# Windowed attention and a two-layer MLP on one core: the first two batches in thirds of 192 tokens, the first chunk up-projected in two column halves, the last 64 tokens loaded ahead of w_in

## The chip, the cores and the metric

The kernel runs on one core of one Trainium2 chip. The metric is the device time of one execution in microseconds (us). TensorE is called PE here, VectorE DVE, ScalarE ACT, GpSimd POOL, and SyncE, whose queue issues nearly all DMAs, SP. PE has two rows in the profile: PE for matmuls and PEld for loads of weights.

## What is computed

Attention over 8 batches, 8 heads, 576 tokens and 64 elements per head, in float32 inputs and outputs. Heads 0 to 3 see a plain window of the last 32 tokens; heads 4 to 7 see a dilated one, every fourth of the last 128. The rows of all heads of a token, side by side (512 wide), then pass an up-projection, a leaky ReLU and a down-projection.

```python
    mask_plain = (rel >= 0) & (rel < window)                                   # window = 32
    mask_dil = (rel >= 0) & (rel < window * dilation) & (rel % dilation == 0)  # dilation = 4
    masks = np.stack([mask_plain if h < H // 2 else mask_dil for h in range(H)], axis=0)
    scores = np.where(masks[None, :, :, :], scale * np.matmul(q, k.transpose(0, 1, 3, 2)), -1e9)
    attn = softmax(scores)
    x = np.matmul(attn, v).transpose(0, 2, 1, 3).reshape(B * S, H * D)         # 4608 x 512
    h = x @ w_in                                                              # 512 x 2048
    return np.maximum(0.01 * h, h) @ w_out                                     # 2048 x 512
```

## The kernel before

**Who sets the order.** No engine's order is written by hand. Every piece of work is a task with an engine (or a choice of engines), a cost, a latency, what it depends on, and a due time or rank (`add`, `dma`, lines 68 to 78). `_Plan.run` (line 85) plays the tasks through a small model and emits each engine's instructions in the order that comes out; for loads the model has a transfer rate by packet size (`took`, 252) and extra lateness (`LATE`). At run time each engine takes its instructions strictly in that order and waits on semaphores, so a task that is not ready holds up all that is behind it. Where the model leaves PE without work early on, filler matmuls on zeros are put in (line 1595; eight more stand at the very start, 1489).

**Loads.** `FIRST` (line 21) ranks the early loads. `b` and `v` are q with k, and v, of one half of the heads of batch 0 (dilated heads first), `i` one of eight blocks of w_in (128 rows by 1024 columns, 512 KB), `o` one of eight blocks of w_out, `0` the last 64 tokens of batch 0, `c`, `y` and `1` the same three things for batch 1. The loads of q, k and v of these two batches hold 512 tokens, four consecutive tokens of a head to a partition; the last 64 tokens come separately (`load_rest`, 501). A DMA may be issued only when the one eight before it has landed. Loaded float32 is cast to float16 by POOL, DVE or ACT (`cast`, line 272). Blocks 1 to 4 of w_in are the four row blocks of its first 1024 columns, blocks 5 to 8 those of the other 1024.

**Attention of the first two batches** (`EARLY`). For each pair of heads `turn` (658) transposes q and k through PE (line 692) and DVE or ACT copy the result into a slot (644, 642), q of the two heads block-diagonally. `unit` (807) then does, for a pair of heads and a part of the tokens: scores on PE (a matmul with a bias that holds the mask, 837, and matmuls on the slots, 840 and 854), Exp on ACT (860), values and row sums on PE (892 or 898, and 886, two heads side by side in 64 columns each), Ln and Exp on ACT (930, 932), which give the reciprocal, and a product on DVE (936) that writes x, transposed, into `xt`. A dilated unit u = 0 or 1 takes two of the four residues of the token number modulo 4, 96 positions each (tokens 0 to 383); u = 2 takes all four residues of the last 48 positions. A plain unit takes two tiles of 96 tokens, u = 0, 1, 2. `attend` (1516) runs units 0 and 1 as part 0 and unit 2 as part 1, behind the last 64 tokens. For batch 0 the plain v is brought from four tokens per partition into tiles by permuting matmuls (`permute`, 333; lines 347 and 353).

**Up and down.** The tokens form twelve chunks of 384 columns. Chunk 0 is tokens 0 to 383 of batch 0, chunk 1 the same of batch 1, chunk 2 the last 192 of both. `up` (1081) makes one of 16 column blocks of 128 of the hidden layer for one chunk: four matmuls, one for each row block of w_in (line 1091), into one of two banks `hps`, and a Prelu on ACT that writes `gt` (1102). For chunk 0 each of the four matmuls is a task of its own; chunk 2 is done in two halves of 192 columns, both late. `down` (1264) multiplies by w_out into the banks `fps` (1275). Later chunks use products of fewer multiplications (1188, 1364), and batches 2 to 7 another attention (`late_unit`, 945).

Of the kernel before, what the change touches and what calls it, by code (L numbers as in the profile page):

```python
# [15 lines left out]
AHEAD, LATE = 5.0, 4.0  # L16
WHEN = (-5.0, 15.0, 46.0, 70.0, 100.0, 126.0, 160.0, 188.0)
CON = -1484.5
LOCK = 60.0
AFTER = -1495.0  # L20
FIRST = "bvbviiii0iiiicoocoyoooooy1"
RANKS = ((10.0, 6.0), (10.0, 0.5), (15.0, 2.0), (25.0, 2.0))


def _constants():
# [15 lines left out]
    d2 = (rel2 >= 0) & (rel2 < WIN)  # L41
    bias = np.where(np.concatenate([first, band, band, d0, d2], axis=1), 0.0, -60000.0)
    parts = [ident, bias, first, band, band, d0, d1, d1, d0, d2]
# [18 lines left out]
class _Plan:  # L62
# [22 lines left out]
    def run(self):  # L85
        free, waiting, lock = {}, {}, {}
        server = 0.0
# [12 lines left out]
        while len(order) < len(self.tasks):  # L100
            best = None
            for eng, cand in waiting.items():
# [3 lines left out]
                if eng == "SP":  # L106
                    here = max(here, server - AHEAD)
# [18 lines left out]
            if t.service:  # L126
                begin = max(at + t.dur + 0.9, server)
                server = begin + t.service
                t.done = server + 1.1 + t.late
            else:  # L130
                t.done = at + t.dur + t.lat
# [11 lines left out]
def kernel(  # L143
# [24 lines left out]
    TILED = ((0, 0), (0, 1), (1, 0))  # L168
    BY_PE = ((0, 0), (0, 1), (1, 0))
    POOL_MASK = (1,)  # L170
    BLOCKS = tuple(range(16))
    N_UPS = 8
# [20 lines left out]
    NBIAS, NMASK = 288 + 96 + 48, 288 + 288 + 48  # L193
# [3 lines left out]
    B_PL, B_D0, B_D2 = 128, 128 + 288, 128 + 288 + 96  # L197
# [47 lines left out]
    tpk = fps[1].bitcast(FP16)  # L245
# [6 lines left out]
    def took(n, size):  # L252
        for a, ta, b, tb in ((4, 9.0, 128, 15.0), (128, 15.0, 256, 19.0), (256, 19.0, 1024, 48.0),
                             (1024, 48.0, 2048, 85.0)):
            if size <= b:
                return n * (ta + (tb - ta) * (size - a) / (b - a)) / 16e3
        return n * size / 25.6 / 16e3

    def load(queue, dst, src, n, size, deps, prio, slow=1.0):
# [3 lines left out]
                        LATE if prio > -1500 + len(FIRST) else 0.8 if prio >= AFTER else 0.0)  # L263
# [35 lines left out]
    def clear_slots(slots, prio, deps):  # L299
        for i in slots:  # L300
            t_zero[i] = ([clear("DVE", qbd[i][64:128, 0:S], 0.34, 0.0, prio, deps),
                          clear("DVE", qbd[i][0:64, S:2 * S], 0.34, 0.0, prio, deps)],
                         [clear("DVE", kt[i][:, 0:PAD], 0.1, 0.0, prio, deps)])

    clear_slots(range(4), -2000, [])
    t_one = clear("POOL", ones, 0.1, 1.0, -1995)
    t_ones = {}
    TWO_ONES = float(np.ones(2, np.float16).view(np.float32)[0])

    def clear_ones(slots, deps, prio=-700):  # L310
        for i in slots:
            t_ones["d", i] = clear("POOL", at(vd[i].bitcast(FP32), 0, 128, D // 2, [64, 16], [1, D // 2]),
                                   0.48, TWO_ONES, prio,
                                   deps)
            t_ones["p", i] = clear("POOL", at(vp[i].bitcast(FP32), 0, 128, D // 2, [64, 12], [1, D // 2]),
                                   0.38, TWO_ONES, prio,
                                   deps)

    clear_ones(range(2), [], -1980)
    t_vr = [clear("POOL", vst[i][0:64, 1024:2048], 1.0, 0.0, -1970 + i) for i in range(2)]  # L320
    SPREAD, SHIFT = 36, 67

    def ident_at(tl, off, step, prio):
        t = clear("DVE", tl.bitcast(FP32), 0.3, 0.0, prio)
        return add("DVE", 0.2, 0.2, [t, t_id], lambda e: nc.vector.tensor_copy(
            out=at(tl, 0, 128, off, [step, 128]), in_=ident), prio)

    t_spread = ident_at(el[0], SPREAD, 4, -1985)
    t_shift = ident_at(el[1], SHIFT, 1, -1600)
    v_half = pair1  # L330
    permuted = []

    def permute(tiles, deps, prio, rest_from=None):

        if rest_from is None:
            n, b_users = tiles[0] // 2, []
            b_old = rings["TPK"][-1] if n else []
            bk = fps[n]
        else:
            n, b_old = ring("F", 2, b_users := [])  # L340
            bk = fps[n]

        def pe(e):
            for y, t in enumerate(tiles):
                for r in range(4):
                    s = 96 * t - 32 - r + SPREAD
                    nc.tensor.matmul(bk[:, 256 * y:256 * y + 256], el[0][:, s:s + 128],  # L347
                                     at(v_half, 0, 128, r * D, [256, 4], [1, D]),
# [309 lines left out]
    def turn(b, hp, part, prio):  # L658
# [89 lines left out]
        else:  # L748
# [39 lines left out]
            if b:  # L788
                ev += q_users
# [863 lines left out]
```

## Time and profile before

| | us |
|---|---|
| median of 3 runs (lowest, highest) | 306.11 (305.94, 306.44) |
| the profiled execution's own time | 306.29 |
| its span (first to last instruction) | 304.5 |
| PE, DVE, ACT, POOL busy | 294.4, 231.0, 188.7, 132.3 |
| HBM read, written | 41.13 MB, 9.44 MB |

In lines of the profile, "L1091 PE MATMUL hps<-xt,w_in" is an instruction from line 1091 on PE that writes the tile hps from xt and w_in. What stands in brackets behind a timeline's line is the time for which the engine had been idle and what released it. PE's busy time runs from the start of a matmul to its modelled end, and matmuls overlap, so the step from one to the next is read from their starts or from the chain of waits. The view of stretches lists, after the length, busy time and instructions of PE, PEld, DVE, ACT and POOL, the granted PE clock, the share of the DMA engines and GB/s.

### The profile page before, as it was taken

The page shows a single profiled execution, that of the slowest core. Times are in us where ns is not written, and L with a number is a line of the kernel's source. Part 1 is how long each engine was busy: PE and PEld are TensorE (multiplying, and loading weights), DVE is VectorE, ACT ScalarE, POOL GpSimd, SP SyncE. Part 2 cuts the span into 40 slices and gives each one's busy share as a digit, 9 for nine tenths or more (in the row PEclk, how much of TensorE's full clock was granted, in tenths as well). Part 3 has the DMA queues.
Part 4 walks back from the last instruction along what each step waited for, and adds up shares of the span by engine and source line. Part 5 has one row for each costly group of instructions (what it writes and reads, how often), then busy time and mean ns, then how long its engine had stood idle before and what let it go on. Part 6 is the DMA issues. An engine that isn't in the chain of part 4 may idle for free.

```text
span 304.5 us, 7869 instructions
## 1 busy us (share of the span) xinstructions
PE 294.4 (97%) x2970; PEld 225.4 (74%) x2970; DVE 231.0 (76%) x478; ACT 188.7 (62%) x458; POOL 132.3 (43%) x179
## 2 busy tenths in 40 slices
PE   6889999999999999997999999999999999999994
PEld 3646655667777676786777777887788999999984
DVE  6875875689686869959888779879775899697552
ACT  3857854795556678464766567456565688767230
POOL 5469555393674949159094668665000000000000
PEclk9999999999999999999999999999999999999999
DMA  7999999999999899976999969793102110031124
GB/s 241 404 370 392 407 289 201 239 201 167 253 171 196 190 188 196 174 180 134 183 161 221 204 136 194 159 208 80 37 2 72 34 37 2 11 91 32 32 76 146
DMA packets 160390, 51.09 MB, mean 168 GB/s; under 512 B 137632, under 2 KB 157024, under 8 KB 160352
## 3 DMA queue, kind: packets, MB, share of 16 engines
q1 hardware_dynamic: 159520, 49.86, 68.3%
q10 hardware_dynamic: 832, 0.73, 0.8%
q8 instruction: 23, 0.38, 0.5%
q14 instruction: 15, 0.12, 0.1%
HBM read 41.13 MB, written 9.44 MB: 166 GB/s over the span
## 4 chain that ended last, share of the span: by engine, by line
PE 90%; DVE 5%; ACT 3%; DMA 1%; issue 1%; DVEq 0%
PE hps L1091 29%; PE fps L1364 26%; PE fps L1275 9%; PE ops L1015 3%; PE hps L1188 3%; PE ops L1188 3%; PE ops L1063 2%; PE sps L1188 2%; PE tp L1188 1%; PE tp L692 1%; PE ops L1364 1%; PE tp L982 1%; PE sps L982 1%; DVE ee L1008 1%; PE fps L347 1%; PE tp L975 1%
## 5 line engine op out<-in xcount | busy, mean ns | idle before, releaser
L1091 PE MATMUL hps<-xt,w_in 128*128 128x384 f16 (+1 forms) x640 | 111.7, 310 | 0.8 <-DVE w_in L272 0.6
L1102 ACT ACTIVATE gt<-hps 128x384 f16<-128x384 f32 (+1 forms) x160 | 72.8, 461 | 43.8 <-PE hps L1091 41.5
L1091 PEld LDWEIGHTS <-w_in 128*128 128x128 f16 x640 | 56.7, 98 | 26.3 <-DVE w_in L272 1.0
L1364 PEld LDWEIGHTS <-gt 128*128 128x128 f16 x672 | 64.4, 98 | 9.7
L679 POOL COPY slots<-turned 64x576 f16<-64x576 f16 x48 | 36.3, 757 | 47.4 <-DVE turned L674 45.5
L1364 PE MATMUL fps<-w_out,gt 128*128 128x256 f16 x416 | 53.6, 273 | 0.0
L272 POOL CAST nat<-stg 128x576 f16<-128x576 f32 (+1 forms) x53 | 43.0, 834 | 9.7 <-DMA stg<-in_q_dram 3.5
L1275 PE MATMUL fps<-w_out,gt 128*128 128x512 f16 x128 | 32.4, 379 | 0.0
L1037 DVE TENSOR_TENSOR rc<-ops,recs 96x384 f16<-96x384 f32 x48 | 25.7, 538 | 0.3
L1393 ACT COPY stg<-fps 128x512 f32<-128x512 f32 (+1 forms) x24 | 12.8, 532 | 14.4 <-PE fps L1364 14.4
L1008 DVE TENSOR_TENSOR ee<-ee,con 128x576 f16<-128x576 f16 x24 | 17.2, 722 | 3.5 <-ACT ee L994 3.5
L1033 DVE RECIPROCAL recs<-ops 96x6 f32<-96x6 f32 x48 | 8.7, 181 | 14.7 <-PE ops L1015 12.5
L1401 DVE TENSOR_TENSOR osb<-fps,stg 128x512 f32<-128x512 f32 x18 | 12.4, 687 | 9.7 <-PE fps L1364 5.6
L272 POOL CAST vd<-v_all 128x1024 f16<-128x1024 f32 (+2 forms) x20 | 18.0, 918 | 2.7 <-DMA v_all<-in_v_dram 2.7
L1211 ACT ACTIVATE gt<-stg 128x384 f16<-128x384 f32 x36 | 18.0, 524 | 1.1 <-DVE stg L1205 1.1
L1275 PEld LDWEIGHTS <-gt 128*128 128x128 f16 x128 | 11.6, 98 | 9.1
L644 DVE COPY slots<-tp 64x128 f16<-64x128 f16 (+7 forms) x42 | 13.4, 333 | 6.3 <-PE tp L692 5.6
L674 DVE STREAM_TRANSPOSE turned<-nat 128x576 f16<-128x576 f16 x24 | 17.7, 751 | 0.0
L685 DVE STREAM_TRANSPOSE slots<-nat 128x576 f16<-128x576 f16 x24 | 17.7, 745 | 0.0
L1008 DVE TENSOR_TENSOR el<-el,con 128x576 f16<-128x576 f16 x24 | 15.0, 630 | 2.7 <-ACT el L994 2.5
L1188 PEld LDWEIGHTS <-w_in 128*128 128x128 f16 x192 | 16.4, 98 | 0.5 <-DVE w_in L1119 0.3
L994 ACT ACTIVATE ee<-sps 128x288 f16<-128x288 f32 x24 | 9.8, 409 | 8.4 <-PE sps L982 5.8
(158 smaller groups left out, 529.3 us busy)
## 6 DMA issues: line engine op xcount, KB each, us to landing
stg<-in_q_dram SPq DMA_DIRECT2D x48, 144.0 KB, 3.2
stg<-in_k_dram SPq DMA_DIRECT2D x48, 144.0 KB, 2.9
v_all<-in_v_dram SPq DMA_DIRECT2D x24, 256.0 KB, 3.8
v_all<-in_v_dram SPq DMA_DIRECT2D x24, 192.0 KB, 3.2
gt<-in_moe_w_in_dram SPq DMA_DIRECT2D x5, 512.0 KB, 7.1
out_dram<-osb SPq DMA_DIRECT2D x22, 96.0 KB, 2.0
out_dram<-osb SPq DMA_DIRECT2D x40, 48.0 KB, 1.8
out_dram<-osb SPq DMA_DIRECT2D x25, 64.0 KB, 2.2
```

Of the source, the lines that this page charges most:

```text
L272: ENG[e].tensor_copy(out=dst, in_=src)
L674: lambda e: nc.vector.transpose(xb, na[:, 0:S]), prio)
L679: lambda e, p0=p0, hh=hh: nc.gpsimd.tensor_copy(out=at(qb, p0, p0 + 64, hh * S + o, *od), in_=at(xb, p0, p0 + 64, i, *id_)), prio, 0.0, "m ...
L685: lambda e: nc.vector.transpose(kb[:, PAD:PAD + S], na[:, S:2 * S]), prio)
L1008: nc.vector.tensor_tensor(out=x, in0=x, in1=mk, op=ALU.mult)
L1037: nc.vector.tensor_tensor(out=at(xb, 0, 96, 768 * n + 64 * i, [256, 3], [128, 2], [1, D]), in0=at(ot, 0, 96, 0, [130, 3], [65, 2], [1, D]) ...
L1091: nc.tensor.matmul(ht[:, 0:n], at(w_in, 0, 128, i * DFF + j // 2 * 256 + j % 2, [2, 128]), at(xt[m % 2], 0, 128, i * 1152 + x0, *dims), st ...
L1102: lambda e: nc.scalar.activation(out=gt[c % NG][:, j * n_c + x:j * n_c + x + n], in_=ht[:, 0:n], func=AF.Prelu, alpha=0.01),
L1188: nc.tensor.matmul(cell[:, n * z:n * z + n], lhs(2 * p + z, i), rhs(i), start=first and z == 0 and i == 0, stop=z == 1 and i == 1, skip_gr ...
L1211: lambda e: nc.scalar.activation(out=at(g, 0, 128, j * n_c + n * y, [n_c, 2], [1, n]), in_=at(src, 0, 128, 0, [n, 2], [1, n]), func=AF.Pre ...
L1275: nc.tensor.matmul(ft, g[:, j * n_c + tt * 128:j * n_c + tt * 128 + 128], w_out[:, j * DM:j * DM + DM], start=(j == 0), stop=(j == NJ - 1))
L1364: nc.tensor.matmul(bk[:, x:x + HN], tl[:, off + j * step:off + j * step + 128], rhs(j), start=first and x == 0 and j == 0, stop=j == HJ - ...
```

## The change

- **Units of 192 tokens.** The first two batches run in three thirds, t = 0, 1, 2 (`attend_third`). A dilated unit now always takes all four residues of 48 positions (four score matmuls of 96 columns instead of two of 192, eight value matmuls of 48 columns instead of four of 96); plain units keep their tiles. q lies in its slot by residue for plain heads too, so that its copies are alike. The loads of 512 tokens and of the last 64 are the same in size; the rows of the last 64 are listed in another order. In both batches the mask is added by PE for all but the last third of batch 1, as before.
- **The first chunk in two halves.** `up_half` makes two column blocks (a pair p of eight) for 192 columns of the chunk in one bank, with one eviction; the first half needs only the first third of batch 0. Chunk 2 uses it too, and its first half is due much earlier.
- **Load order.** `FIRST` puts the last 64 tokens of batch 0 (`0`) ahead of all eight blocks of w_in.
- **Banks and clears.** A second bank for scores of thirds 1 and 2 is `fps0`; transposes and permutes of batch 0 alternate between two banks; two tiles' tails are taken from one spread identity.
- **The planner's constants** change: rates of `took`, lateness (4.0 to 2.5 for late loads, 0.8 to 0.3 for early ones), no factor 1.3 on the first blocks of w_in, and a limit of eight DMAs in flight early on.

The diff, cut to its core:

```diff
-AHEAD, LATE = 5.0, 4.0
+AHEAD, LATE = 5.0, 2.5
-FIRST = "bvbviiii0iiiicoocoyoooooy1"
-RANKS = ((10.0, 6.0), (10.0, 0.5), (15.0, 2.0), (25.0, 2.0))
+FLIGHT = 8
+FIRST = "bvaw0iiiiiiiicooeoyooooox1"
+LOADS = {"b": (0, 1, False), "v": (0, 1, True), "a": (0, 0, False), "w": (0, 0, True),
+         "c": (1, 1, False), "y": (1, 1, True), "e": (1, 0, False), "x": (1, 0, True)}
+RANKS = ((-30.0, 5.0), (-8.0, 0.1), (-6.0, 0.1), (-4.0, 0.1), (-3.0, 0.1), (20.0, 2.0))
...
-    BY_PE = ((0, 0), (0, 1), (1, 0))
+    BY_PE = ((0, 0), (0, 1), (0, 2), (1, 0), (1, 1))
-    BLOCKS = tuple(range(16))
-    N_UPS = 8
+    banks["S1"] = banks["S"] + fps[:1]
...
-        u_lo, u_hi = ((0, 96) if u < 2 else (96, 144)) if dil else (48 * u, 48 * u + 48)
+        u_lo, u_hi = 48 * u, 48 * u + 48
-            key = (chunk_at(m, base), b % 2 if b < EARLY and lo >= 96 else 0)
+            key = (chunk_at(m, base), b if u == 2 else u if b == 0 else 0)
...
+            if dil:
                 for s in range(4):
                     nc.tensor.matmul(
                         st[:, 96 * s:96 * s + 96],
                         at(kb, 0, 128, s * 144, [1, 128]),
-                        at(qb, 0, 128, s * 144 + 96, [S, 2], [1, 48]),
+                        at(qb, 0, 128, s * 144 + 48 * u, [S, 2], [1, 48]),
...
-                    qa = at(qb, 0, 128, 96 * t, [S, 2], [1, 96])
+                qa = at(qb, 0, 128, 24 * t, [S, 2], [144, 4], [1, 24])
...
+    def up_half(c, y, p, done, acc):
+        hn, h_old = ring("H", len(hps), h_users := [])
+        ht, ts = hps[hn], [None]
+        def part_of(i):
+            def fn(e):
+                for z in range(2):
+                    nc.tensor.matmul(ht[:, 192 * z:192 * z + 192],
+                                     at(w_in, 0, 128, i * DFF + p * 256 + z, [2, 128]),
+                                     at(xt[0], 0, 128, i * 1152 + x0, *x_in),
+                                     start=(i == 0 and z == 0), stop=(i == NI - 1 and z == 1),
+                                     skip_group_check=True)
+            return fn
+        for i in range(NI):
+            ts.append(add("PE", 0.166, 0.25 * (i == NI - 1),
+                          done + w_in_t[2 * p][:i + 1] + h_old + ts[-1:], part_of(i),
+                          UP_AT[c][y] + 0.65 * p, 0.0, "U"))
+        t_a = add("ACT", 0.39, 0.22, ts[-1:] + gt_free.get(c - NG, []),
...
+    UP_AT = {0: (0.0, 5.2), 2: (12.0, 45.0)}
+    UPS = (((0, 0, 0),), ((0, 0, 4), (0, 1, 0), (0, 1, 4)), ((2, 0, 0), (2, 0, 4)))
...
+                for t in range(3):
+                    attend_third(b, t, *RANKS[3 * b + t])
...
+                    if b == 0:
+                        for c, y, p in [(c, y, p) for c, y, p0 in UPS[t] for p in range(p0, p0 + 4)]:
+                            acts = all_acts.setdefault(c, [[] for _ in range(NJ)])
+                            up_half(c, y, p, x_done[c, y], acts)
```

## Prediction

> **What bounds the kernel now.** I read the busy time by stretches first, then TensorE's own timeline over the first 24 us, then the casts that release it, then the chain of waits for the price of each piece of TensorE work.
>
> The stretches (us; PE is busy time and instructions):
>
> ```profile
> 0.00:20.00 20.00, 16.39 (x147) 9.68 (x147) 15.61 (x49) 12.31 (x32) 10.21 (x23) 1.00 0.94 330
> 20.00:100.00 80.00, 79.16 (x762) 51.96 (x761) 57.49 (x133) 52.07 (x141) 50.56 (x72) 1.00 1.02 256
> 100.00:200.00 100.00, 98.23 (x1021) 74.95 (x1020) 83.58 (x154) 63.46 (x148) 64.35 (x77) 1.00 0.88 178
> 200.00:300.70 100.70, 100.65 (x1046) 88.85 (x1044) 73.91 (x143) 60.91 (x138) 7.22 (x10) 1.00 0.23 57
> 300.70:304.50 3.80, 0.00 (x0) 0.00 (x0) 0.42 (x1) 0.00 (x0) 0.00 (x0) 0.98 0.39 124
> ```
>
> PE (first column after the length) is full from 20 us to 300.7 but for under 3 us; then 3.8 us of stores end the span. So the end moves only by (a) PE time lost before it saturates, (b) the amount of PE work, (c) new holes later. The timeline of PE shows where (a) ends:
>
> ```profile
> 18.00 1.25 PE L1595 MATMUL fps<-warm 128*128 128x512 f16 x5
> 19.09 1.16 PE L1091 MATMUL hps<-xt,w_in 128*128 128x384 f16 x6
> 20.89 0.50 PE L1091 MATMUL hps<-xt,w_in 128*128 128x384 f16 x2 [0.64 <-DVE w_in L272]
> 21.22 0.38 PE L1595 MATMUL fps<-warm 128*128 128x512 f16 x1
> 21.80 1.46 PE L1091 MATMUL hps<-xt,w_in 128*128 128x384 f16 x8 [0.20 <-ACT gt L1102]
> ```
>
> L1595 is filler on zeros. PE waits for the fourth block of w_in: no column group can stop without all four row blocks. From 21.80 nothing is missing. POOL's timeline dates the landings, since POOL idles until each block lands:
>
> ```profile
> 13.48 0.61 POOL L272 CAST w_in<-gt 128x512 f16<-128x512 f32 x1 [0.65 <-DMA gt<-in_moe_w_in_dram]
> 14.76 0.61 POOL L272 CAST w_in<-gt 128x512 f16<-128x512 f32 x1 [0.66 <-DMA gt<-in_moe_w_in_dram]
> 16.04 0.61 POOL L272 CAST w_in<-wst 128x512 f16<-128x512 f32 x1 [0.67 <-DMA wst<-in_moe_w_in_dram]
> 18.96 0.61 POOL L272 CAST w_in<-wst 128x512 f16<-128x512 f32 x1 [1.84 <-DMA wst<-in_moe_w_in_dram]
> ```
>
> One block takes 1.28 us of a saturated DMA (16.04 - 14.76). The chain of waits gives PE's prices:
>
> ```profile
> 23.26 0.45 PE tp L692 x8
> 23.71 1.30 PE hps L1091 x8
> 25.01 0.16 PE sps L837
> 25.17 0.17 PE sps L840 x4
> ...
> 26.64 0.87 PE fps L347 x8
> 27.52 0.55 PE fps L353 x8
> ...
> 30.57 0.24 PE ops L892 x8
> 30.80 0.09 PE ops L886 x2
> 30.89 0.27 PE sps L837
> ```
>
> So 8 transposes 0.45; 8 up-projection matmuls of 384 columns 1.30; a score unit 0.33; 8 permuting matmuls 0.87, their 64-row tail 0.55. A value unit of four 48-column pairs costs 0.24 + 0.09 + (0.27 - 0.16) = 0.44; one of two 96-column pairs (0.21 + 0.08 + 0.11 at 32.75 in the same view) 0.40. An up-projection group of 8 x 192 columns is 0.66 (75.64 there).
>
> **The change, part by part.**
>
> *PE time lost before saturation, old.* By 21.80 PE has done 32 transposes (1.8), 8 score units (2.6), 8 value units (3.2), 16 permuting matmuls (1.75) and 8 matmuls of up-projection (1.3): 10.65. Lost: 21.80 - 10.65 = **11.15 us**.
>
> *Loads.* The first ten are the same; the v that ends them lands at 12.2 (POOL's cast of it starts at 12.22). Before, four blocks of w_in follow, with the four small loads of the last 64 tokens behind; the last of these lands at 12.23 + 7.3 = 19.5. All eight took 7.3 us, of which the blocks need 4 x 1.28 = 5.1, so the small ones cost 2.2. Now they go first: block 1 lands at 12.2 + 2.2 + 1.28 = 15.7 instead of 13.4, and block 4 at 19.5 instead of 18.9. Bounds for block 4: 18.9 (its old time) to 20.1 (0.6 later). SP issues the same loads behind it in the same order up to the 47th, so blocks 5 to 8 (landings up to 25.1) and all of w_out stay where they are.
>
> *PE time lost, new.* The changed kernel's instruction order puts ahead of the fourth block: 40 transposes (2.25, the small ones of the last 64 tokens are now among them), 8 score units (2.65), 6 value units, four of 48 columns (2.55), all 24 permuting matmuls with their tail (3.15), and 6 of the 8 matmuls of the first half group (0.5): 11.1. Is PE there in time? The plain half of the first third ends late: v cast 12.8 to 13.3, permute, its copy, values near 15.8, then ACT's Ln and Exp and DVE's product (0.33, 0.36, 0.34) behind casts of w_in: near 18; then one more value unit; PE arrives near 19.7. Block 4 is cast in 0.42 on DVE (as at 18.47) and free at 20.1. Lost there: 20.1 - 11.1 = 9.0.
>
> That cast is the first place for a rule. In DVE's timeline it takes 0.42 us with POOL idle (18.47), but 0.97 at 16.43 and 1.16 at 19.67 with POOL at work. The sum above takes 0.42. The Trainium skill (SBUF — State Buffer, Who interferes with whom) says that such a cast and a GpSimd instruction hold one shared pair of ports as an exclusive lock, the later one blocking fully; the trace agrees (0.97 and 1.16). By it, POOL's half of the same block would hold DVE back some 0.6 us, which speaks against a change that moves PE closer to this cast; the sum stays, as the next wait takes in those 0.6 us.
>
> *The next wait.* From 20.1 PE has column pairs 0 to 3 of the first half, two value and two score units and half of pair 4: 3.9 us, to 24.0. Then pair 4 needs block 7, cast by POOL alone, and behind that matmul stand in PE's order two value units, two score units and later the second half's pairs 0 to 3, which are ready and cannot pass. POOL: block 4's half to 20.4, clears of el (0.7, as at 28.20 and 29.16), a cast of v (0.7, as 26.27), blocks 5 and 6 (1.16 each, 21.25 on), then half of block 7: 24.7. Stall 0.7; bounds 0 and 2.7 (POOL two us later). Lost: 9.7.
>
> *More PE work.* Dilated units go from 96 to 48 columns: 8 of them, 8 x 0.04 = 0.3. The first chunk's 64 matmuls become 128 of half the width, 16 x 0.01 = 0.16. Scores, permutes and transposes keep their columns. Plain scores now read runs of 24 elements; no row shows that, between 0 and 2.0 (12 tiled units, 0.165 each, at half speed); I take 0, as the strided runs of 48 (L886) stream at full rate. Together 0.5.
>
> *Free elsewhere.* The third chunk's halves are evicted two column blocks at a time, DVE has fewer small copies: ACT is 62% busy, DVE 76%, PE is not held by either after 21.80 except 0.17 and 1.60 us (121.8 and 142.55). These may go or come back elsewhere: 0 taken, -1.6 to +1.6. The last 700 matmuls stand in the same order, so the 3.8 us at the end stay.
>
> **Sum**: 11.15 - 9.7 - 0.5 = 0.95 us gained. The profiled execution took 306.29 us (span 304.5), so 305.3; the median of the runs is 0.18 lower, so **305.2 us**. A measurement of this kernel tells about 0.2% (0.6 us) from no change.
>
> **Rivals.**
> - *ACT takes the gain back: 306.1, chance 0.20.* Only two banks serve the up-projection. From 20 to 31 us ACT now has 16 evictions (0.42 apart), 4 exponentials (0.39) and 6 pairs of Ln and Exp (0.62): 12 of about 14.5 us, since two pairs slid behind the fourth block. For: PE already waited 0.20 for gt at 21.80. Against: that is the only such wait. At 0.15 per pair, 0.9 us: no change.
> - *POOL's queue decides and it is slower: 307.2, chance 0.22.* One mechanism: pairs 4 to 7 of the first half stand ahead of ready work, and each us that POOL casts blocks 7 and 8 later than PE gets there is a us of the end. Two us later than my reckoning give 0.95 - 2.0 = 1.05 lost; it turns slower from a slip of 1.0. For: POOL has clears and a cast of v ahead of block 5, and is idle nowhere from 20 to 27. Against: the landings alone (16.00 + 7.8 = 23.8 for block 7) would have it cast by 24.4.
> - *No stall at block 7 and the 1.6 us of 142.55 gone: 303.2, or one of both: about 304; together 0.13.*
> - *A cold PE: 307, chance 0.03.* The first eight fillers took 604 ns each, later ones 381. Fillers fall from 22 to 13, and none stands behind the third score unit. If the work before 20 us ran at half speed, 3 us of it doubled would arrive 1.7 us late. The Trainium skill (TensorE: Matmul & The Clock Gate, What's actually happening) has the clock halve after an idle window of about 3.4 us; the granted clock here is 1.00 in every stretch, and my reckoning has no hole over 1.3 us.
> - The forecast itself, 304.5 to 305.5: 0.42.
>
> Faster by over 0.2%: 0.42 + 0.13 = 0.55; within: 0.20; slower: 0.25. **Range** 303.2 to 307.2: both outer rivals' prices; what is beyond them is under 2 in 10.
>
> **What would show it.** Right: POOL's first w_in cast near 15.7, the last of the first four near 19.5; PE's first stop of an up-projection near 20.2; one hole of under 1 us near 24 ended by POOL's w_in cast; none over 0.3 from 26 to 100 us. Wrong: PE waiting on DVE or ACT at the first up-projection (the third's chain, not w_in, is late); several holes before hps ended by ACT; a w_in cast by POOL after 25.5 for block 7; new holes after 100 us larger than 1.8 in sum.

## The result and the profile after

| | median us (lowest to highest, runs) | ratio to before, 95% interval |
|---|---|---|
| before | 306.06 (305.57 to 307.22, 13) | |
| after | 309.52 (306.53 to 310.65, 13) | 1.0095 [1.0069, 1.0121] |

The change makes the kernel about 1% slower; the forecast was 305.2, in a range of 303.2 to 307.2. The medians and ranges here are over all runs; a ratio leaves out runs that lie more than 1.5% above their kernel's fastest.

What the ratio does not tell is the spread: before stays within 1.7 us, after covers 4.1, and its profiled execution (306.53 us, span 304.8) is the fastest of the thirteen. A profile of it alone explains the wrong kernel. Four of the thirteen runs had a mean granted clock of 0.998 or more (306.53, 307.41, 309.10 and 309.17 us), the other nine 0.994 or less (307.13 to 310.65). The stretches of the profiled execution:

```profile
0.00:20.00 20.00, 15.31 (x153) 9.42 (x154) 13.18 (x37) 13.65 (x31) 9.27 (x21) 1.00 0.93 333
20.00:100.00 80.00, 79.57 (x870) 56.50 (x871) 60.72 (x137) 54.41 (x136) 52.94 (x75) 1.00 1.00 251
100.00:200.00 100.00, 98.37 (x1011) 74.19 (x1008) 79.22 (x151) 62.03 (x144) 61.76 (x75) 1.00 0.94 190
200.00:300.70 100.70, 100.66 (x1048) 89.08 (x1046) 72.09 (x143) 60.18 (x138) 3.80 (x5) 1.00 0.18 48
300.70:304.80 4.10, 0.39 (x4) 0.10 (x1) 0.42 (x1) 0.00 (x0) 0.00 (x0) 1.00 0.45 138
```

PE is again full from 20 us on, at clock 1.00. Its timeline there, with DVE's behind it:

```profile
20.80 1.76 PE L1024 MATMUL hps<-xt,w_in 128*128 128x192 f16 x16
22.91 0.28 PE L806 MATMUL ops<-ee,vp 128*64 128x96 f16 x4 [0.34 <-DVE xt L844]
23.20 0.83 PE L1024 MATMUL hps<-xt,w_in 128*128 128x192 f16 x8
24.25 0.34 PE L1024 MATMUL hps<-xt,w_in 128*128 128x192 f16 x2
```

```profile
19.33 0.76 DVE L273 CAST w_in<-wst 128x512 f16<-128x512 f32 x1
20.20 1.02 DVE L277 MEMSET slots<- 64x288 uint32 x3
21.15 0.35 DVE L273 CAST w_in<-wst 128x512 f16<-128x512 f32 x1
```

The first up-projection starts at 20.80 and works for the first third's columns while the second third is still in work, as the change intends; DVE casts the last needed half block at 21.15, behind three clears. There is no hole from 23 to 162 us.

To say what moved, each moment of PE up to its last matmul is put into one of three parts, from the starts and ends in the trace (where two matmuls overlap, the later one has the moment): its own work, time lost before 30 us (fillers and holes), and holes after 30 us. A trace lacks a few matmuls, so the own work is good to some 0.4 us.

| execution | lost before 30 us | own work | holes after 30 us | last matmul ends |
|---|---|---|---|---|
| before, 306.29 us | 11.48 | 287.39 | 1.81 | 300.69 |
| after, 306.53 us | 10.12 | 289.30 | 1.67 | 301.09 |
| after on another chip (e15), 312.00 us | 10.19 | 292.07 | 4.14 | 306.39 |

In the fastest execution the early gain is there (1.36 us; 1.45 was forecast) and more work eats it. The common execution has two things more: work that takes longer, and longer holes. The experiments separate them.

### The profile page after: what moved, and what is told of

The parts are those of the page before. It is cut to its first block, busy times and chain, and to the rows that moved or that the text cites. A ratio compares the mean times of both kernels' runs of the same rounds, so it can differ in the third digit from the quotient of the medians.

```text
span 304.8 us, 8057 instructions
## 1 busy us (share of the span) xinstructions
PE 294.3 (97%) x3073; PEld 229.3 (75%) x3073; DVE 225.6 (74%) x467; ACT 190.3 (62%) x448; POOL 127.8 (42%) x174
## 4 chain that ended last, share of the span: by engine, by line
PE 84%; POOL 4%; DMA 4%; DVE 3%; ACT 2%; SPq 2%; issue 1%; POOLq 0%; DVEq 0%
PE fps L1302 22%; PE hps L998 19%; PE fps L1211 9%; PE hps L1024 7%; PE hps L1124 3%; PE ops L1124 3%; DMA v_all<-in_v_dram 3%; PE ops L923 3%; POOL slots L540 2%; PE sps L1124 2%; PE ops L971 2%; SPq L263 2%; PE tp L1124 1%; PE fps L1427 1%; PE ops L1302 1%
## 5 line engine op out<-in xcount | busy, mean ns | idle before, releaser
L998 PE MATMUL hps<-xt,w_in 128*128 128x384 f16 x448 | 86.7, 326 | 0.0
L1005 ACT ACTIVATE gt<-hps 128x384 f16<-128x384 f32 x112 | 55.4, 494 | 34.1 <-PE hps L998 31.6
L998 PEld LDWEIGHTS <-w_in 128*128 128x128 f16 x448 | 40.4, 98 | 20.2
L540 POOL COPY slots<-turned 64x576 f16<-64x576 f16 x48 | 40.3, 840 | 20.3 <-DVE turned L535 18.7
L273 POOL CAST nat<-stg 128x576 f16<-128x576 f32 (+1 forms) x52 | 36.8, 732 | 23.4 <-DMA stg<-in_q_dram 15.9
L1024 PE MATMUL hps<-xt,w_in 128*128 128x192 f16 x256 | 25.7, 246 | 0.1
L1024 PEld LDWEIGHTS <-w_in 128*128 128x128 f16 x256 | 20.6, 98 | 1.5 <-DVE w_in L273 0.3
L273 POOL CAST vd<-v_all 128x1024 f16<-128x1024 f32 (+2 forms) x18 | 16.7, 935 | 8.7 <-issue 3.9
L1035 ACT ACTIVATE gt<-hps 128x384 f16<-128x384 f32 x32 | 15.7, 490 | 5.3 <-PE hps L1024 4.9
L273 POOL CAST vp<-v_all 128x768 f16<-128x768 f32 x14 | 14.3, 1023 | 10.4 <-DMA v_all<-in_v_dram 9.5
L1124 PEld LDWEIGHTS <-w_in 128*128 128x128 f16 x192 | 16.4, 98 | 0.5 <-DVE w_in L1055 0.3
```

The costliest lines, as they stand in the source:

```text
L273: ENG[e].tensor_copy(out=dst, in_=src)
L540: lambda e, p0=p0, hh=hh: nc.gpsimd.tensor_copy(out=at(qb, p0, p0 + 64, hh * S + o, *od), in_=at(xb, p0, p0 + 64, i, *id_)), prio, 0.0, "m ...
L998: nc.tensor.matmul(ht[:, 0:n], at(w_in, 0, 128, i * DFF + j // 2 * 256 + j % 2, [2, 128]), at(xt[m % 2], 0, 128, i * 1152 + x0, *dims), st ...
L1005: lambda e: nc.scalar.activation(out=gt[c % NG][:, j * n_c + x:j * n_c + x + n], in_=ht[:, 0:n], func=AF.Prelu, alpha=0.01),
L1024: nc.tensor.matmul(ht[:, 192 * z:192 * z + 192], at(w_in, 0, 128, i * DFF + p * 256 + z, [2, 128]), at(xt[0], 0, 128, i * 1152 + x0, *x_in ...
L1124: nc.tensor.matmul(cell[:, n * z:n * z + n], lhs(2 * p + z, i), rhs(i), start=first and z == 0 and i == 0, stop=z == 1 and i == 1, skip_gr ...
```

## The experiments

A number of chips took part, and the changed kernel differs between them (medians of 309.5 and 311.1, and a single run of 313.6), so only runs beside each other are compared; each set stands beside its own runs of before. In the expectations, theory A is that the granted clock falls in the thin early stretch, theory B that the loss lies in the later loads and the order laid for them, theory P that the planner's new price of loads is what spoils that order.

### First set: is it the clock, and does it come with the fillers?

e1 is the changed kernel unchanged. e2 is the kernel before without its 14 fillers at L1595:

```diff
-        while t.start > 0.5 and x + 0.3 < u.start:
+        while False and t.start > 0.5 and x + 0.3 < u.start:
```

e3 is the changed kernel with the last 64 tokens back behind four blocks of w_in:

```diff
-FIRST = "bvaw0iiiiiiiicooeoyooooox1"
+FIRST = "bvawiiii0iiiicooeoyooooox1"
```

> The changed kernel, unchanged, for a second profile: its one profile so far (span 304.8, granted clock 1.00) is the fastest of 13 runs, ten of which took 309.0 to 310.7 with granted clocks of 0.987 to 0.999. Theory A (PE falls to half clock somewhere in the thin stretch ahead of the first up-projection, since the fillers that stood there are gone): span 307 to 309 in most such runs, the row of the granted clock below 9 in one of the slices before 25 us, matmuls there at twice their duration, and PE full again only 2 to 4 us later than the 23.2 us of the first profile. Rival B (a wait in the middle of the run, on DVE and POOL, that comes and goes): full clock, holes of 2 us or more after 100 us. Rival C (loads or the chain of the first third vary): full clock, first up-projection 2 to 4 us later than 20.8 us, ended by DMA or ACT.

> The kernel before without the 14 filler matmuls between its own matmuls (the eight at the very start stay). Nothing else differs. Theory A: the clock falls here too, 308 to 310 us in most runs, granted clock under 1. Rivals B and C: fillers are idle time, so 306.1 us as before, within 0.3.

> The changed kernel with one part undone: the last 64 tokens of batch 0 are loaded behind the first four blocks of w_in again, and the order of the engines follows. Theory A: no filler comes back, so the slow runs stay, median near 309.5. Rival C with the loads as cause: w_in is there 2 us earlier, median back to 306 to 307. If the price of the load order is what I reckoned before (nothing by itself, since the fourth block lands at nearly the same time), within 0.6 us of the changed kernel.

Measured beside before (305.69): e1 313.55 (one run); e2 308.02 (305.85 to 310.67), 1.0051 [1.0013, 1.0090]; e3 311.46 (308.91 to 312.89), 1.0196 [1.0139, 1.0253]. Taking only fillers from the kernel before makes it slower: the three of e2's ten runs with a mean clock of 1.000 took 305.85 to 306.34, as before does, the seven with 0.994 or less 306.59 to 310.67.

Its profiled run (310.67) has the same order as before, so the two can be set side by side, instruction by instruction on ACT. It is 1.7 us late at 12.9 us, 2.0 at 18.5, 4.0 at 28.4 and 4.4 at the end. The second rise lies around a fall of the clock to 0.50 from 23.5 to 26.9 us. The first is half clock too (the loads are not late: v lands at 12.29 against 12.17), though the clock column does not show it: the trace's record of the clock begins only at 13.28 us, and four transposes take 0.61 us ahead of that and 0.38 behind it (in before the record begins at 3.98 us):

```profile
12.79 0.61 PE L692 MATMUL fps<-con,nat 128*128 128x128 f16 x4
14.07 0.38 PE L692 MATMUL fps<-con,nat 128*128 128x128 f16 x4 [0.16 <-ACT slots L642]
```

The old load order does not mend the changed kernel. The clock's fall can be dated; stretches of e3, then of e1, early and late:

```profile
10.20:13.60 3.40, 1.88 (x37) 1.47 (x38) 2.30 (x6) 2.83 (x8) 0.94 (x2) 1.00 1.03 398
13.60:17.00 3.40, 2.91 (x16) 1.84 (x14) 1.09 (x2) 2.45 (x5) 1.51 (x3) 0.50 1.03 403
17.00:20.40 3.40, 3.01 (x45) 2.26 (x44) 2.64 (x7) 2.77 (x10) 2.98 (x5) 1.00 1.06 333
```

```profile
14.95:18.35 3.40, 3.40 (x21) 2.37 (x20) 1.08 (x3) 1.83 (x5) 1.81 (x4) 0.50 1.03 410
164.10:167.50 3.40, 0.00 (x0) 0.00 (x0) 3.02 (x8) 0.00 (x0) 3.11 (x5) 1.00 1.09 287
168.60:172.00 3.40, 3.40 (x20) 2.04 (x20) 2.33 (x4) 1.46 (x4) 3.34 (x3) 0.50 0.96 150
172.00:175.40 3.40, 3.40 (x31) 2.63 (x29) 3.33 (x8) 1.92 (x5) 3.10 (x4) 1.00 0.86 164
```

The last column but two is the granted clock: 0.50 for one stretch of 3.4 us, in which PE is busy for 2.9 us or more and issues 16 to 21 matmuls where 31 and more follow. At half speed 3.4 us cost at most 1.7 us. Beside after, whose order it shares, e1 is level at 11.6 us and 1.6 us late from 19.4 to 157 us (the first four blocks of w_in also land 0.9 to 2.1 us later there, so this need not all be the clock); it is 5.1 us late at 169 us, 6.4 at 179 and 7.0 at the end. e1 has two falls: one after the thin stretch, one after a hole of 3.53 us near 165 us. That hole is the second cause:

```profile
163.00 1.04 PE L1302 MATMUL fps<-w_out,gt 128*128 128x256 f16 x8
167.57 0.36 PE L923 MATMUL ops<-vp,ee 128*128 128x65 f16 x6 [3.53 <-DVE ee L916]
168.52 0.38 PE L883 MATMUL sps<-slots 128*128 128x192 f16 x2 [0.59 <-POOL slots L540]
```

```profile
159.85 1.27 POOL L273 CAST nat<-stg 128x576 f16<-128x576 f32 x2 [2.95 <-DMA stg<-in_k_dram]
163.78 1.28 POOL L273 CAST nat<-stg 128x576 f16<-128x576 f32 x2 [2.66 <-DMA stg<-in_k_dram]
165.00 0.69 POOL L540 COPY slots<-turned 64x576 f16<-64x576 f16 x1
```

PE names DVE and POOL, but DVE waits for POOL's cast and POOL for the load of k: the loads of batch 6 come too late for the place that its first visit (the first scores of that batch) has in PE's order.

### Second set: fillers back, and lateness added

e4 is the changed kernel with ten more zero matmuls in PE's holes from 11 to 15 us, on hps0, which is free until its first values:

```diff
-    taken = [(t.start, max(x.done for x in t.users)) for t in in_spare]
+    taken = [(t.start, max(x.done for x in t.users if x.n == t.n + 1)) for t in in_spare]
...
+            to = spare
             if spare is fps[0] and any(y < x + step and x < z for y, z in taken):
-                x += 0.1
-                continue
-            w = _Task((("PE", step),), 0.0, [], idle(n, spare), 0, 0.0, 0, "w")
+                if x > 15.0:
+                    x += 0.1
+                    continue
+                to = hps[0]
+            w = _Task((("PE", step),), 0.0, [], idle(n, to), 0, 0.0, 0, "w")
...
+    i = pe.index(permuted[0][0])
+    for u, many in zip(pe[i - 4:i], (1, 2, 0, 3)):
+        for _ in range(many):
+            w = _Task((("PE", 0.0),), 0.0, [], idle(512, hps[0]), 0, 0.0, 0, "w")
+            w.eng, w.start, w.dur, w.done = "PE", u.start - 0.001, 0.0, u.start
+            order.append(w)
```

e5 adds 1.75 us of pure lateness to e4, e6 adds the same to the kernel before:

```diff
+    late = [t for t in pe if t.kind == "U"][8]
+    for _ in range(8):
+        w = _Task((("PE", 0.0),), 0.0, [], idle(512, fps[0]), 0, 0.0, 0, "w")
+        w.eng, w.start, w.dur, w.done = "PE", late.start - 0.001, 0.0, late.start
+        order.append(w)
```

e7 is e4 without the column halves' head start (the first chunk waits for both thirds):

```diff
-    UPS = (((0, 0, 0),), ((0, 0, 4), (0, 1, 0), (0, 1, 4)), ((2, 0, 0), (2, 0, 4)))
+    UPS = ((), ((0, 0, 0), (0, 0, 4), (0, 1, 0), (0, 1, 4)), ((2, 0, 0), (2, 0, 4)))
...
-                            up_half(c, y, p, x_done[c, y], acts)
+                            up_half(c, y, p, x_done[c, 0] + x_done[c, 1] if c == 0 else x_done[c, y], acts)
```

> The changed kernel with ten more zero matmuls (on bank hps0, which nothing uses before 15 us) put into the holes of TensorE between 11 and 15 us; nothing else differs. Theory A (the granted clock falls to a half for one window of 3.3 us after the thin stretch 11 to 15, and the lateness grows further down): clock 0.997 or more in nearly every run, median 306.2 to 307.0, as the one undisturbed run of the changed kernel (306.53). Rival B (the loss lies in the later load stream or in the new order, whatever the clock does): median stays at 309 to 310. Rival C (the zero matmuls delay TensorE's own work): 307.5 or more with the clock at 1.00.

> The kernel of e4 with eight more zero matmuls of 512 columns behind the first eight matmuls of up-projection, near 21 us, when TensorE has no idle time: 8 x 0.22 = 1.75 us of pure lateness at full clock. Theory A1 (in the changed kernel lateness of 1.7 us is amplified, as the stores that SP waits for stand ahead of the loads of later batches and a hole opens near 163 us): 3 to 6 us over e4. Rival (lateness is only passed on): 1.7 us over e4, no more than 1 us of holes near 163.

> The kernel before with the same eight zero matmuls behind its first eight matmuls of up-projection. If lateness is only passed on: 305.9 + 1.7 = 307.6. If the load stream amplifies lateness in the kernel before too: 309 or more. If amplification is a property of the new order alone: 307.6 here and more than that in e5.

> The kernel of e4 in which the first chunk's up-projection waits for both thirds (all 384 columns) as before, though still computed in two halves; the planner then puts more zero matmuls into the wait. If the split is what feeds TensorE from 21 us on: first up-projection near 24 us instead of 20.8, 2 to 4 us over e4. Rival (the split gives nothing, since the second third's columns are ready as early as the blocks of w_in): within 0.7 us of e4.

| beside before 306.04 | median us (range) | ratio |
|---|---|---|
| e4 | 311.02 (308.89 to 312.45) | 1.0182 [1.0158, 1.0205] |
| e5 | 310.80 (309.25 to 311.05) | 1.0141 [1.0117, 1.0166] |
| e6 | 307.83 (307.51 to 307.89) | 1.0056 [1.0043, 1.0069] |
| e7 | 311.99 (311.06 to 312.80) | 1.0194 [1.0171, 1.0217] |

Theory A alone falls: with the fillers the clock is 1.00 from 5 us to the last matmul of its profiled run, and e4 still takes 311.0, two of its five runs (311.02 and 312.02) with a mean clock of 1.000. My fear that lateness is amplified falls too, and in a telling way. In the kernel before 1.75 us of PE time are 1.8 us at the end: PE is the bound. On top of e4 the same 1.75 us cost nothing: there PE waits later for loads anyway, and comes to them no later than they do. The profiled runs agree, with 2.04 us of holes after 30 us in e5 and 3.30 in e4; but two of e4's runs fell to a clock of 0.987 and none of e5's did, a part of the difference that is not separated. e7's profiled run (312.2 us) has a hole of 1.91 us that ends at 23.5, where up-projection of the first third would have stood, starts up-projection at 27.3 (24 was expected), loses 13.23 us before 30 us against e4's 11.21, and runs at half clock from 24.3 to 31.1. So the head start is worth some 2 us of early loss and keeps the clock up; that the median is only 1.0 us above e4, and not 2 to 4, would fit e5, since e4 waits for loads later. The order after 30 us differs too, so these sizes are rough.

### Third set: how much cover the planner gives to loads

LATE is the time that the planner adds to the landing of each later load; the change cut it from 4.0 to 2.5, and in after the slots of batch 6's first visit are copied 0.1 us before PE uses them, in before 4.3 us. So I put it back (e8; e9 with e4's fillers), went beyond (e11, 6.0), and gave the kernel before the new value (e10). PE's first 597 matmuls keep their order in e8.

```diff
-AHEAD, LATE = 5.0, 2.5
+AHEAD, LATE = 5.0, 4.0
```

> The changed kernel with one constant of the planner put back: LATE, the time it adds to the landing of each later load, 4.0 us instead of 2.5. The order of the first 40 us stays as it is. Theory B (the change cut the planned cover of the later loads; the slots of batch 6 now come 0.1 us after TensorE could use them, 4.3 us before it in the kernel before, so every lateness of the load stream goes to the end): holes near 163 us gone or below 0.5 us, spread of the runs smaller, median 307.0 to 308.5, of which the part above 306.5 is the half clock of one window in most runs. Rival A (half clock at 12 to 18 us and what follows from it is all): no change, 309.5. Rival C (holes only move elsewhere): 309 or more with holes at other places.

> As e8, with the ten zero matmuls of e4. If both causes are real and add: 306.0 to 307.2 with clock 0.997 or more and little spread. If only the load stream counts: as e8. If the ten matmuls do harm: above e8.

> The kernel before with LATE at 2.5, as the changed kernel has it, and nothing else. Theory B: slack of its tightest visits falls by about 1.5 us, holes between 100 and 200 us, 307 to 309 with more spread. Rival: within 0.2% of before, and the loss of slack comes from another part of the change.

> The changed kernel with LATE at 6.0, more than either kernel had. Theory B: no holes that wait on loads; median at or a little below e8 (306.5 to 308). Rival (the cover costs elsewhere, as TensorE's order has nothing to put ahead of the late visits): above e8.

| beside before 305.77 | median us (range) | ratio |
|---|---|---|
| e8 | 310.62 (310.25 to 315.59) | 1.0161 [1.0134, 1.0188] |
| e9 | 313.40 (311.53 to 316.08) | 1.0252 [1.0212, 1.0291] |
| e10 | 304.18 (303.51 to 304.37) | 0.9936 [0.9918, 0.9954] |
| e11 | 314.59 (311.02 to 315.27) | 1.0254 [1.0213, 1.0296] |

Theory B's figure misses in all four. For e8 and e11 the rivals came out (holes at other places; cover that costs elsewhere), e9 lies above e8 as if the fillers did harm, and e10 lies outside both its forecasts. More LATE does not mend the changed kernel, and less makes the kernel before faster than both kernels: a part of the change that is a gain by itself, at least in this one order. e10's stretch from 100 to 200 us has no hole left, where before had 1.60 us at 142.55:

```profile
100.00:200.00 100.00, 100.00 (x1047) 76.72 (x1046) 81.47 (x159) 64.84 (x151) 60.72 (x76) 1.00 0.88 177
200.00:298.80 98.80, 98.73 (x1028) 87.47 (x1025) 72.40 (x142) 58.85 (x134) 5.79 (x8) 1.00 0.24 61
```

### Fourth set: the planner's price of loads

The planner computes a landing for every DMA of SP. Set against the real landings (DMAs 1 to 332 in SP's order; real less planned, us; the planned landing is taken without the LATE that the planner adds for loads), the kernels fall into two kinds:

| execution | 115th | 155th | 179th | 203rd |
|---|---|---|---|---|
| before | -5.6 | -4.0 | -1.9 | -2.1 |
| e10 | -3.9 | -2.9 | -0.8 | -1.7 |
| after | 2.0 | 3.2 | 7.4 | 8.4 |
| e15, after on another chip | 1.9 | 4.7 | 7.8 | 9.8 |

In before the loads come ahead of the dates for which PE's order was laid; in after they come 7 to 10 us behind from the 179th on (5 to 7 when the 2.5 us of LATE are allowed for), at clock 1.00 as well. It is not PE that is late: ACT's instructions, most of which follow PE, are 1.3 to 2.0 us behind the plan all the way from 27 to 153 us in after, while the landings slip from 0.6 us behind at the 60th DMA to 7.4 at the 179th. The change had lowered the price of rows of 128 and 256 bytes in `took`, and from batch 2 on q and k come in rows of 128 bytes and the plain heads' v in rows of 256. A load of q or k has 1,152 such rows, so the planner counts 0.12 us less for each ((15.0 - 13.3) x 1152 / 16 ns); 81 of them, and 20 of v at 0.03, lie ahead of the 203rd DMA: 10.6 us. e12 and e13 (with e4's fillers) put the old price back, e14 puts the new one into the kernel before:

```diff
-        for a, ta, b, tb in ((4, 9.0, 128, 13.3), (128, 13.3, 256, 18.3), (256, 18.3, 1024, 48.5),
+        for a, ta, b, tb in ((4, 9.0, 128, 15.0), (128, 15.0, 256, 19.0), (256, 19.0, 1024, 48.5),
```

> The changed kernel with the planner's old price for rows of 128 and 256 bytes (15.0 and 19.0 instead of 13.3 and 18.3); TensorE's first 1,036 rows stay as they are. Theory P (the lower price laid the later visits against loads that come 7 to 9 us after their planned dates): holes after 30 us below 1 us in all, real landings near 160 to 200 us within 3 us of the planned ones, spread of the runs small; median 305.0 to 306.5 where the half clock comes in most runs, 303.5 to 305 where it does not. Rival (the price has nothing to do with it, and the order moves holes at random): 308 to 311.

> e12 with the ten zero matmuls of e4. If the half clock at 12 to 18 us is worth its 1.5 us and holes are gone: clock 0.997 or more, 0.5 to 1.5 us below e12's median, spread under 1 us. If the ten matmuls cost what they cure: as e12.

> The kernel before with the new price for rows of 128 and 256 bytes (13.3 and 18.3), LATE at 4.0 and all else as it is. Theory P: the same harm as in the changed kernel, holes of 2 us and more between 75 and 205 us, 308 to 311 with a spread of 2 us, at a clock of 0.997 or more in its first 30 us. Rival: within 0.5% of before.

Measured beside before (305.97): e12 308.40 (307.11 to 309.75), 1.0070 [1.0046, 1.0094]; e13 307.44 (306.73 to 308.46), 1.0044 [1.0028, 1.0061]; e14 306.77 (304.97 to 311.74), 0.9999 [0.9978, 1.0019].

e14 does not reach theory P's 308 to 311: by its median it is 0.8 us above before, by the mean of all twelve runs 1.5, by the ratio level with it, as the rival had it. What the price alone does there is the lateness and the spread: its 203rd DMA lands 8.9 us behind its date, 11.0 later than in before, while ACT keeps within 0.6 us of the plan from 21 to 170 us; and the kernel that kept within 1.3 us beside it now covers 6.8. In its profiled run (309.02 us) a hole opens at the same visit; that its runs of 305 to 306 us had their loads in time is likely, but none of them was traced. PE and POOL of the profiled run:

```profile
171.48 1.04 PE L1364 MATMUL fps<-v_all,gt 128*128 128x256 f16 x8
176.18 0.28 PE L975 MATMUL sps<-slots 128*128 128x192 f16 x2 [3.66 <-POOL slots L679]
```

```profile
170.73 1.89 POOL L272 CAST nat<-stg 128x576 f16<-128x576 f32 x3 [2.09 <-DMA stg<-in_k_dram]
174.54 0.83 POOL L272 CAST vp<-v_all 128x768 f16<-128x768 f32 x1 [1.93 <-DMA v_all<-in_v_dram]
175.44 0.69 POOL L679 COPY slots<-turned 64x576 f16<-64x576 f16 x1
```

Here POOL copies the slot only after two waits for loads. e12 came out some 2 us above what theory P gave, and its 179th and 203rd DMA still land 4.3 and 4.1 us behind, so the price is not all of it there. A hole of 1.8 us that ends at 143.7 remains in e12 and e13; a product on DVE ahead of it takes 3.39 us in e13, as one of 2.95 us stands ahead of the hole of before.

### Fifth set: the table of four, on one chip

e15 is the changed kernel, e16 that of e12, e17 that of e4 and e18 that of e13.

> The changed kernel itself, as the corner of the table of four. If price and half clock are both real: 309 to 313 with a spread of 3 us and more, clock 0.994 or less in most runs.

> The changed kernel with the old price of e12. If the price carries most of the loss: 2 to 4 us below e15, clock still 0.994 in most runs. If the half clock carries it: within 1 us of e15.

> The changed kernel with the ten zero matmuls of e4. If the price carries most of the loss: within 1.5 us of e15, with the clock at 0.997 or more except where a long hole comes later. If the half clock carries it: 2 to 4 us below e15.

> Both. If they add: e15 less the sum of the two differences, near 306.8 to 307.6, spread under 2 us. It stays above before by the 1.4 us that more TensorE work (1.9 us) and less early loss (0.75 us) leave.

| beside before 306.29 | median us (range) | ratio | runs with clock under 0.996 |
|---|---|---|---|
| e15: after | 311.09 (308.82 to 312.00) | 1.0140 [1.0109, 1.0170] | 5 of 6 |
| e16: old price | 308.04 (306.81 to 311.63) | 1.0067 [1.0042, 1.0092] | 6 of 8 |
| e17: fillers | 309.55 (307.16 to 311.48) | 1.0116 [1.0076, 1.0155] | 1 of 6 |
| e18: both | 307.06 (306.45 to 307.35) | 1.0027 [1.0011, 1.0042] | 0 of 8 |

By the medians the price is worth 3.05 us (2.49 with the fillers in), the fillers 1.54 (0.98 once the price is right), both 4.03: nearly a sum, and the spread falls from 3.2 us to 0.9. By the means over all runs it is 2.0 (2.6) for the price, 1.0 (1.6) for the fillers and 3.6 for both. The price and the pair are clear of the noise; the fillers by themselves are not, as the intervals of e15 and e17 overlap. The two runs of e16 whose clock stayed up took 306.81 and 307.38, as e18 does. In e16 and e18 batch 6's first visit has 4.2 us of cover again, and the 203rd DMA of e16 lands 1.1 us from its date, that of e18 1.3. In e15's profiled run a hole of 2.19 us ends at 205.1; POOL had waited 3.90 us for a load of k ahead of it. The half clock in e15, then the same stretches with fillers in e18:

```profile
10.90:14.30 3.40, 1.38 (x14) 0.85 (x12) 2.40 (x6) 2.90 (x8) 0.99 (x2) 1.00 1.09 329
14.30:17.70 3.40, 2.98 (x17) 2.24 (x18) 0.69 (x2) 2.00 (x6) 2.39 (x4) 0.50 1.03 410
```

```profile
10.90:14.30 3.40, 3.06 (x26) 1.62 (x24) 2.27 (x6) 2.90 (x8) 0.61 (x1) 1.00 1.07 294
14.30:17.70 3.40, 3.35 (x48) 2.48 (x46) 1.58 (x4) 2.88 (x8) 2.58 (x4) 1.00 1.03 402
```

and what it does to one group, the eight permuting matmuls of e15, which took 1.04 us in after and in e18:

```profile
15.01 1.91 PE L342 MATMUL tp<-pair,el 128*128 128x256 f16 x8
```

e18 still stands 0.8 us above before. By the three parts, its early loss is 11.35 us (before 11.48), its holes after 30 us are 1.86 (1.81), its own work is 288.26 (287.39): what is left of the change is the added work.

## Why the prediction was wrong

**"Free elsewhere": the failed step.** It priced ACT's and DVE's copies behind 30 us and took 0, between -1.6 and +1.6 us. It did not price the planner's constants at all, though the order after 30 us is laid with them. Of them the price of loads alone is 3.05 us in the table of four (2.0 by the means). The cue was in the code, not in the profile: a lower price moves every later visit ahead, and whether real loads follow can be read by setting the plan's landings against the trace's. I had the trace of before, in which loads came 2 to 6 us ahead of the plan; the price cut, 0.12 us on each of 81 loads and 10.6 us in all, could be had from the diff and uses this up. That it is the price, and not just another shuffle of the order, rests on the slip of the landings, which both kernels show with the new price and much less (e12, e16) or not at all (before) with the old, and on one order for each case; e8 to e11 show that other edits of the planner move the time as far.

**"A cold PE: 307, chance 0.03": the right mechanism, far too small a chance.** The price was given as 1.7 us; it is 1.0 to 1.6 in the table of four. The rule that I leaned on was that the clock falls after an idle window, and "my reckoning has no hole over 1.3 us" holds: the largest hole between 9 and 15 us is 0.91. But in e15 the clock fell behind 3.4 us in which PE was busy for 1.38, in e3 behind 1.88 of 3.4. The Trainium skill (TensorE: Matmul & The Clock Gate, What's actually happening) gives one idle window of about 3.4 us as the condition; the length agrees with every trace here, the condition doesn't: thin is enough. It also says that the window runs freely, which agrees with one order falling in one execution and not in the next: after's profiled run had 1.27 busy of 3.4 (11.4 to 14.8) and kept its clock, but the steps of its own clock record, a whole number of 3.413 us from the first, cut that stretch in two:

```profile
8.85:12.27 3.42, 2.67 (x44) 1.67 (x42) 2.44 (x7) 2.45 (x8) 0.53 (x1) 1.00 1.13 391
12.27:15.68 3.41, 1.73 (x17) 1.42 (x18) 1.66 (x4) 2.89 (x7) 2.23 (x4) 1.00 1.00 336
```

Fillers had fallen from 22 to 13, I had seen it, and asked only how long the longest hole is.

**Early loss: 9.7 forecast, 10.12 in the profiled run, 11.35 in e18.** The old one was 11.15 by my reckoning, 11.48 by the table. So of the gain of 1.45 us that was forecast, the profiled run shows 1.36, e16's (no fillers, clock up) 0.54 and e18's 0.13: that it came out in the first was largely luck. Its terms:
- *Loads.* The small loads took 1.83 us (v at 11.68, the last small one at 13.51), not 2.2. Block 4 was forecast at 19.5, within 18.9 to 20.1. It landed at 18.53 in the profiled run, at 18.77 in e11, at 19.27 in e15, and at 20.1 to 21.4 in the eleven other traces with this load order. The bounds were too narrow on both sides.
- *"PE arrives near 19.7".* It started at 20.80. The third's plain half was later than I had it: its permute started at 15.00, not 13.35, since ACT made its last two casts of q and k at 11.14 and 11.91, behind Ln and Exp of the first units, and the second score unit waited 0.91 us for DVE's copy. So DVE's and ACT's copies ended PE's holes up to 15 us; "the third's chain, not w_in, is late" was the sign named for being wrong.
- *Stall at block 7, 0.7.* It did not come: no hole from 23 to 162 us in the profiled run. POOL's casts were in time, as PE came 1.1 us later than I had it.
- The lock on DVE's cast (0.42 or 0.97 us) decided nothing in the profiled run: the last cast took 0.35, but stood behind clears in DVE's order, which I had not looked for. In seven other traces (e4, e5, e9, e12, e16, e17, e18) it may have: the DVE cast ahead of those clears, beside casts and clears on POOL, took 1.47 to 1.97 us where after's took 0.76, and PE then stood 0.75 to 0.89 us for w_in from 21.4 to 21.9 us on.

**More work: 0.5 forecast, 0.9 to 1.9 measured.** By groups in after against before: scores with their bias 8.21 us against 7.84, values and sums 6.73 against 6.23, up-projection 95.17 against 94.82; together 1.2. I had given nothing to scores and to the first half's strided columns.

**Put together.** In the fifth set after lies 4.80 us above before where 0.95 below was forecast, 5.75 off. By the medians the price and the fillers are 4.03 of it, the early gain that is missing in e18 1.32 (0.13 for 1.45), the added work 0.37 (0.87 for 0.5). With both causes mended the change is still no gain.

**The other rivals.** ACT's evictions did not hold PE (no hole before hps ended by ACT after 20 us). POOL's queue did not slip. The hole at 142.55 went in after, as one rival had it, but its place was taken by those at 162 to 183.

**Still open.** Why a longer LATE made the changed kernel no faster (e8) or slower (e9, e11) is not settled: the new orders had holes at 78 to 90 us and at 164 to 201 us, but I did not separate these from the chip's own spread. In e8 and e9 the slots of batch 6's first visit still come only 0.05 us before their use, and the 203rd DMA lands 12.4 and 11.0 us behind its date (after: 8.4), so 1.5 us more of LATE did not buy cover there; in e11 (16.6 us behind) the visit has 5.05 us, and holes of over 2 us stand at 162 and 199. Why the changed kernel differs by 2 us between chips (4 with e1's single run) while before doesn't was not tested; that its end hangs on landings, which vary from run to run, while that of before hangs on PE (e6) would explain it.

## What to carry to other kernels

When an order is laid by a planner, a change of its prices is a change of the whole kernel: set the planned landings against those of the trace before asking what the rest of the change does. Fillers that keep PE's clock up are part of the schedule; count PE's busy time in every 3.4 us of an early stretch, and where it falls under 2 us, give half clock a real chance, not a residue (it came behind 12 of 28 such windows here). And where the runs of a kernel spread over 1%, the profile of one of them, above all the fastest, is no picture of its median.

## What was not expected of the hardware

In all twenty traces the clock record changes only at whole multiples of 3.413 us from its first entry. Cut there, 28 windows ahead of the last matmul have PE busy for less than 2.0 us at full clock. Behind 12 of them the clock fell, for one window (for two in e7): these had 0.41 to 1.89 us of PE time. Behind 16 it did not, with 1.38 to 1.99 (before's thinnest has 1.81, 140.5 to 143.9). All six under 1.38 fell; from there to 1.89 busy time alone does not decide, and what does is open.

Ahead of the first entry of that record the clock column shows 1.00, but matmuls step at half speed: 128 columns take 107 ns up to 13.2 us in e2 and 55 behind. The first entry lies between 3.6 and 13.3 us in the twenty traces (3.98 in before, 5.44 in after). So "1.00 in every stretch", as the prediction read it, leaves out the start.

The DMAs carry more than the kernel's own bytes. In after's view of DMA queues:

```profile
q8 instruction: 24, 0.39, 0.5%
q14 instruction: 15, 0.12, 0.1%
```

The packets of q8 are 16 KB each and occupy one DMA engine for 0.9 to 1.6 us. One came at 18.57 us, and the block of w_in behind it landed 2.68 us after the one ahead instead of 1.28; in before one came at 16.01, ahead of the block that took 2.92. The fourteen traces with the changed load order have exactly one such gap each (1.83 to 2.83 us, the other steps between blocks 1.12 to 1.31), and the first packet of q8 starts within 1 us of where that gap begins. In after, e11 and e15 the gap lies behind block 4, which landed at 18.5 to 19.3 us; in the other eleven it lies ahead of it. That the packets cause this was not tested.
